# An RWKV-7 layer with a squared-ReLU feed-forward: stores of N on ScalarE's queue, moves of tokens three steps later, and v of chunk 5 fetched with its r

## The chip, the cores and the metric

The kernel runs on one core of one Trainium2 chip. The metric is the device time of a run in microseconds; the median of three runs is compared. Engines are named as in the profile: PE is TensorE (PEld its weight loads), DVE is VectorE, ACT is ScalarE, POOL is GpSimd, SP is SyncE. ACTq, SPq and POOLq are the sequencers of these engines when they issue DMAs.

## The reference

Four batches, eight heads, 768 time steps, head size 40. Each head has a 40 x 40 state that is updated step by step; its output goes, as 3072 tokens of 320 values, through a feed-forward layer of width 2048.

```python
for t in range(S):                       # S = 768; r, k, v, w, a, b: (4, 8, 768, 40)
    y[:, :, t] = einsum('bhd,bhde->bhe', rt, state)
    Sa = einsum('bhde,bhe->bhd', state, at)
    state = state * wt[:, :, None, :] - einsum('bhd,bhe->bhde', Sa, bt) + einsum('bhd,bhe->bhde', vt, kt)
x = y.transpose(0, 2, 1, 3).reshape(3072, 320)
h = maximum(x @ w_in, 0)                 # w_in (320, 2048)
out = (h * h) @ w_out                    # w_out (2048, 320)
```

## The kernel before

The sequence is cut into chunks of 128 steps; with four batches there are 24 chunks, in the order batch first, then time (`order`). `B` is 4. Within a chunk the recurrence becomes triangular systems that are solved by a matrix N and the inverse T of its diagonal blocks.

A chunk passes through these stages:

- `early(i)` (L342) reads w, a and b, forms the running products of decay (two scans and two reciprocals on DVE), and makes N: TensorE multiplies into PSUM, and ACT copies the result to the tile N (L373 to L377). The tile N has one buffer (L370), so the next chunk's copies wait until every store of this one has been read. Then N is stored to DRAM for the solver: in four pieces, `kept_q` for chunks 0 to 9 and `kept_d` for the others (L388); for chunks 2 to 9 also `kept_m`, two pieces (L390); for chunks from 2 on also `kept_n` (L392). The decay products go to `kept_e` (L367). Chunks 0 and 1 keep N's block and the decay products in SBUF; two of their four pieces are issued by ACT, everything else by SP.
- `take(u)` and `solve(u)` load the pieces of a unit of one, two or four chunks onto POOL, which solves for T (L448, L450) and stores it as `kept_t`.
- `rest(i)` in the first four slots, or the steps of `sorted_slot` later, loads k, the decay products `dec`, r, v, b, T (as `blocks` while the units are fine), N and `spares`, and forms kvT, A, rT, RV. For the fine units T is completed by two small products whose results ACT copies (`spares` L494, T L501).
- `chain(i)` (L604) is the recurrence itself: xr, two products with T, one with N between them, RX, and the output tile `tokens` (L669). After every second chunk, eight small DMAs (`moves`, L678 to L680) move rows within `tokens`, so that the feed-forward products fill 128 rows; `gathered` (L681) tells that they have been moved.
- The class `Ffn` multiplies tokens with `w_in` in quads (`thirds`, `whole`), squares on DVE and multiplies with `w_out` in quarters. The weights come in as pairs of 32-bit words and are put together by `rounding` (L258 to L277), on ACT and DVE, during the first five slots.

The order of instructions on each engine is written out by hand. A prologue (L827 to L868) prepares chunks 0 to 3. Then there is one slot for each chunk. Slots 0 to 3 use `woven` (L881): a `weave` of 12 steps interleaves the chain of chunk i, one or two `early` of later chunks (`ahead`: 4 and 5 in slot 0, 6 and 7 in slot 1, 8 and 9 in slot 2, 10 in slot 3, 11 and 12 in slot 4, 13 and 14 in slot 5, then one for each slot up to slot 14), `rest(i + 1)` and the rounding. Slots from 4 on use `sorted_slot` (L908), a fixed list of steps. The feed-forward part starts in slot 4.

DMAs that must not stand too early in SP's queue are put on a list with a number of steps:

```python
def later(fn, steps=2):
    line.append([steps, fn])

def tick():
    for entry in line:
        entry[0] -= 1
    while line and line[0][0] <= 0:
        line.pop(0)[1]()
```

`tick` runs once a step. The list is first in, first out: an entry with few steps waits for one with more that stands ahead of it. `store` is `later` with a DMA. `flush` ticks until the list is empty; it stands ahead of each `take`.

`fetch` takes the next tile of a ring: r has one tile, k and b two, v three. Chunk 5's r is fetched in `rest(4)` (L581) and its v at the end of slot 3 (L979), ahead of the other loads for chunk 5 (`loads`, L898). From slot 4 on the v of a chunk is fetched by L953.

Of the kernel before, what the change touches and what calls it, by code (L numbers as in the profile page):

```python
# [17 lines left out]
def kernel(  # L18
# [88 lines left out]
    def store(out_, in_, steps=2, queue=nc.sync):  # L107
        later(lambda: queue.dma_start(out=out_, in_=in_), steps)  # L108
# [233 lines left out]
    def early(i, g=None, apart=False):  # L342

        x_ = early_loaded.pop(i)
        dec = decays.next() if g is None else kept_here[i]
        if g is not None:
            nc.vector.memset(dec[:, :A_, :, MID:MID + 1], 1.0)
        up, down, aT = (dec[:, n] for n in (UP, DOWN, A_))
        wT = turn(x_["w"])
        yield  # L350
        for q in range(NP):
            nc.vector.tensor_tensor_scan(up[:, q, MID + 1:C + 1], wT[:, q, MID:], ones, 1.0, Alu.mult, Alu.mult)  # L352
            nc.vector.tensor_tensor_scan(down[:, q, MID - 1::-1], wT[:, q, MID - 1::-1], ones, 1.0, Alu.mult, Alu.mult)
        yield
        if not apart:
            bT_, aT_ = turn(x_["b"]), turn(x_["a"])
        nc.vector.reciprocal(down[:, :, MID + 1:C + 1], up[:, :, MID + 1:C + 1])  # L357
        nc.vector.reciprocal(up[:, :, :MID], down[:, :, :MID])
        yield
        if apart:  # L360
            bT_, aT_ = turn(x_["b"]), turn(x_["a"])
            yield
        bT = turned("bT", 1)
        nc.vector.tensor_tensor(bT, bT_, down[:, :, 1:C + 1], Alu.mult)
        nc.vector.tensor_tensor(aT[:, :, :C], aT_, up[:, :, :C], Alu.mult)  # L365
        if g is None:
            store(kept_e[i], dec[:USED])  # L367
        yield
        bb, c = order[i]
        t_ = new("N", [128, H, C], 1)  # L370
        for e, p_ in enumerate(products(bT, aT[:, :, :C])):
            plain, flip_ = t_[:, e:NP:2], t_[:, NP + e::2]
            nc.scalar.copy(plain, p_[:, ::2])  # L373
            for half in range(2):
                own_, other = (slice(n * HC, (n + 1) * HC) for n in (half, 1 - half))
                nc.scalar.copy(flip_[own_, :, own_], p_[other, 1::2, other])  # L376
            nc.scalar.copy(flip_[:HC, :, HC:], p_[:HC, 1::2, HC:])  # L377
        joins = lambda half: t_[half * HC:half * HC + Q, :, half * HC + Q:(half + 1) * HC]
        for half in range(2):
            for n in range(2):  # L380
                at = half * HC + n * Q
                if i < SMALL:
                    kept, to = kept_q[i, :, half, n], at + Q
                else:
                    u = unit_of[i]
                    kept, to = kept_d[u][i - units[u][0], :, half], (half + 1) * HC
                    kept = kept[:, n * Q * HC:n * Q * HC + Q * (to - at)].rearrange("h (s t) -> h s t", s=Q)
                store(kept.rearrange("h s t -> s h t"), t_[at:at + Q, :, at:to], 1, nc.scalar if g is not None and n else nc.sync)  # L388
            if i < SMALL and g is None:
                store(kept_m[i][half], joins(half), 1)  # L390
        if g is None:
            store(kept_n[i], t_[:HC, :, HC:], 1)  # L392
        else:
            g["dec"], g["N"] = dec, new("N21", [HC, H, HC], 2)
            nc.scalar.copy(g["N"], t_[:HC, :, HC:])
            g["joins"] = spare("joins", i)
            for half in range(2):
                nc.scalar.copy(g["joins"][half * HC:half * HC + Q], joins(half))
        yield
# [168 lines left out]
    def rest(i, g):  # L568
        begin(i, g)
        yield  # L570
        yield
        turn_k(i, g)
        joining = inverses(i, g) if i else iter(())
        if soon(i):
            next(joining, None)
        yield
        make_a(i, g)
        yield
        turn_rv(i, g)
        if i == B:  # L580
            fetch_next(i + 1, "r")  # L581
        yield
        decay_state(i, g)
        make_rv(i, g)
        if i and unit_of[i] < FINE:
            next(joining)
        yield
        turn_down(i, g)
        yield
        scale_kb(i, g)  # L590
        turn_state(i, g)
        yield
        yield from joining
        yield
# [9 lines left out]
    def chain(i, g):  # L604
        bb, c = order[i]
        st = states.tiles[bb]
        first, second_ = halves
        k_, b_, v_, rT = (g[x] for x in ("k", "b", "v", "rT"))

        x_ = psum(ps_c)[:, :DM].rearrange("t (h d) -> t h d", h=H)  # L610
        if c > 0:
            for f in range(2):
                for q in range(NP):
                    mm(x_[halves[f ^ q % 2], 2 * q:2 * q + 2], g["aT"][:, q, f * HC:(f + 1) * HC], st[:, q, :, :D], f == 0 and q < 2)
        for f in range(2):
            for n, (h, q, e, flip) in enumerate(heads):
                mm(x_[halves[f ^ flip], h], g["A"][e][:, q, f * HC:(f + 1) * HC], v_[:, h, :D], c == 0 and f == 0 and n < 2)
        xr = new("xr", [128, H, D], 1)
        nc.scalar.copy(xr, x_)  # L619
        yield  # L620
        T, N = g["T"], g["N"]
        xn = minus_x.next()

        def times_t(half):
            xs = psum(ps_c)[:, :NP * D].rearrange("p (n d) -> p n d", n=NP)
            for n, (h, q, e, flip) in enumerate(heads):
                rows = halves[half ^ flip]
                mm(xs[rows, n // 2], T[rows, order_of(h)], xr[rows, h], n < 2)
            for flip in range(2):
                nc.scalar.copy(flipped(xn)[halves[half], flip, :, :, :D], by_pair(xs[halves[half ^ flip]]))  # L630

        times_t(0)
        yield
        for h, q, e, flip in heads:
            mm(x_[halves[1 - flip], h], N[:, order_of(h)], xn[first, h, :D], False)
        for flip in range(2):
            nc.scalar.copy(flipped(xr)[halves[1 - flip], flip], flipped(x_)[halves[1 - flip], flip])
        yield
        times_t(1)
        yield  # L640
        p_ = psum(ps_c)
        for q in range(NP):
            nc.tensor.transpose(p_[:, q * 128:(q + 1) * 128], pair(xn, q), ident)  # L643
        xT = turned("xnT", 1)
        nc.scalar.copy(xT, quads(p_))
        yield
        y_ = quads(psum(ps_c))
        if c > 0:
            sd = g["sd"]
            for q in range(NP):  # L650
                mm(y_[:, q], sd[:, q].rearrange("p e d -> p (e d)"), rT[:, q], q == 0)
        yield
        rx = masked("RX", 2, xT, rT)
        yield

        for m_, rows in ((g["RV"], k_), (rx, b_)):
            for q in range(NP):
                for e in range(2):
                    mm(y_[e * DP:(e + 1) * DP, q], rows[:, 2 * q + e, :], m_[e][:, q], c == 0 and q == 0 and rows is k_)
        if c < NCH - 1:  # L660
            grown = psum(ps_w)[:, :NP * D].rearrange("p (q d) -> p q d", q=NP)
            for l_, r_ in ((k_, v_), (b_, xn)):
                for h in range(H):
                    mm(grown[h % 2 * DP:(h % 2 + 1) * DP, h // 2], l_[:, h, :], r_[:, h, :D], l_ is k_ and h < 2)
        n = i % GB
        if n == 0:
            tokens[i // GB] = new("tokens", [128, NP, GB * C], 2)
        t_ = tokens[i // GB][:, :, n * C:(n + 1) * C]
        nc.vector.tensor_tensor(t_, y_, g["up"][:, :, :C], Alu.mult)  # L669
        if c < NCH - 1:  # L670
            for e in range(2):
                rows = slice(e * DP, (e + 1) * DP)
                nc.vector.tensor_tensor(st[rows, :, e, :D], grown[rows], st[rows, :, e, :D], Alu.add)
            ended[bb] = new(f"end{bb}", [128, NP], 1)
            nc.scalar.copy(ended[bb], g["up"][:, :, C])
        if n == GB - 1:
            t_ = tokens[i // GB]
            for j, row, h, d, m_ in moves:  # L678
                at = (h % 2) * DP + d
                store(t_[row:row + m_, j], t_[at:at + m_, h // 2], 1)  # L680
            later(lambda: gathered.add(i // GB), 2)  # L681
        yield


# [283 lines left out]
    for i in range(len(order)):  # L968
# [4 lines left out]
        if i < B:  # L973
# [2 lines left out]
            n["chain"] = chain(i + 1, n)  # L976
            next(n["chain"])
            if i == B - 1:
                fetch_next(i + 2, "v")  # L979
                loads(i + 2)  # L980
        else:
            sorted_slot(i, g, ch)
# [37 lines left out]
```

## Time and profile before

| | us |
|---|---|
| median of 3 runs | 987.36 (986.25 to 987.77) |
| the profiled execution | 987.0 |
| its span | 985.3 |
| TensorE busy in the span | 875.7 (89%) |
| VectorE busy | 485.0 (49%) |
| ScalarE busy | 275.5 (28%) |
| GpSimd busy | 576.1 (58%) |
| SyncE's DMA queue (q1) | 259188 packets, 86.39 MB |
| ScalarE's DMA queue (q10) | 1088 packets, 0.13 MB |

The share of busy time is a mean over a stage of some 330 us in which the kernel loads, rounds and prepares, and a stage in which the feed-forward products fill TensorE. The output tile of the first chunk is written at 95.2 us, that of the last at 910.5 us. A wait in brackets is the idle time of an engine just ahead of an instruction, and what ended it. DMA issues on SPq and ACTq are not counted as busy.

### The profile page before, as it was taken

Reading aid. Unit: us, or ns where it says so; the run is one execution under the profiler, and the core shown is the slowest. Engines: PE = TensorE matmul, PEld = TensorE weight load, DVE = VectorE, ACT = ScalarE, POOL = GpSimd, SP = SyncE. Lnnn points to the kernel's source line nnn. Section 1 sums busy time; section 2 is a strip of 40 time slices with the busy share of each in tenths; the row PEclk is TensorE's granted clock in tenths of the full one; section 3 lists DMA queues with packets and bytes.
Section 4 is the critical chain, followed back from the end, with each engine's and each line's share of the span. In section 5 each row is a group of like instructions: output and inputs, shape, how many; then the busy total and the mean of one; then the engine's idle time right before and its main releaser. Section 6 shows DMA issues by size and latency. Waiting matters only on the chain.

```text
span 985.3 us, 21632 instructions
## 1 busy us (share of the span) xinstructions
PE 875.7 (89%) x8752; PEld 725.8 (74%) x8752; DVE 485.0 (49%) x868; ACT 275.5 (28%) x711; POOL 576.1 (58%) x989
## 2 busy tenths in 40 slices
PE   6447666667897999999999999999999999999998
PEld 4436555556685888888888888888888888887776
DVE  5528775758755454475446655632444423331111
ACT  3132423234323342332223232322222222222111
POOL 4788482836018985999976999959999800000000
PEclk9757565657698999999999999999999999999999
DMA  8987987894667579465588772585404364030000
GB/s 100 143 160 131 191 158 164 171 170 118 91 127 132 100 138 183 92 122 78 97 167 156 124 113 70 102 183 82 66 19 78 82 121 71 14 64 8 14 13 14
DMA packets 263431, 104.16 MB, mean 106 GB/s; under 512 B 246148, under 2 KB 252676, under 8 KB 261924
## 3 DMA queue, kind: packets, MB, share of 16 engines
q1 hardware_dynamic: 259188, 86.39, 50.9%
q0 software_dynamic: 3056, 16.26, 6.9%
q8 instruction: 69, 1.13, 0.5%
q10 hardware_dynamic: 1088, 0.13, 0.1%
q14 instruction: 30, 0.25, 0.1%
HBM read 70.11 MB, written 30.66 MB: 102 GB/s over the span
## 4 chain that ended last, share of the span: by engine, by line
PE 64%; SPq 1%; DVE 1%; DMA 1%; ACT 0%; issue 0%; ACTq 0%
PE ps_f L87 36%; PE ps_w L87 11%; PE ps_c L87 11%; PE ps_w L316 4%; PE ps_c L560 1%; PE ps_c L643 1%; PE ps_w L544 1%; DMA dec<-kept_e 1%; SPq L108 1%; SPq L464 0%; DMA tokens<-tokens 0%; DVE decay L357 0%; DVE state L535 0%; DVE RV L332 0%; ACT N L376 0%
## 5 line engine op out<-in xcount | busy, mean ns | idle before, releaser
L448 POOL TENSOR_TENSOR half_p<-half_n,half_t 128x120 f32<-128x120 f32 (+37 forms) x438 | 255.7, 584 | 84.4 <-DMA half_n<-kept_d 26.5
L450 POOL TENSOR_TENSOR half_t<-half_t,half_p 128x120 f32<-128x120 f32 (+37 forms) x438 | 275.9, 630 | 34.3
L87 PE MATMUL ps_f<-w_out,hid 128*128 128x320 f32 x768 | 217.4, 436 | 0.0
L87 PEld LDWEIGHTS ps_f<-w_out,hid 128*128 128x128 f32 x768 | 142.5, 190 | 54.6 <-issue 0.2
L87 PE MATMUL ps_f<-tokens,w_in 128*128 128x256 f32 x672 | 157.2, 388 | 0.0
L87 PEld LDWEIGHTS ps_f<-tokens,w_in 128*128 128x128 f32 x672 | 126.7, 194 | 17.9 <-issue 1.0
L734 DVE TENSOR_TENSOR hid<-hid 128x512 f32<-128x512 f32 x96 | 88.9, 963 | 50.2 <-ACT hid L727 49.7
L727 ACT ACTIVATE hid<-ps_f 128x512 f32<-128x512 f32 x84 | 50.2, 597 | 96.0 <-PE ps_f L87 96.0
L352 DVE TENSOR_TENSOR_SCAN decay<-ps_w,ones 128x64 f32<-128x64 f32 x88 | 23.8, 271 | 81.5 <-PE ps_w L316 81.5
L669 DVE TENSOR_TENSOR tokens<-ps_c,dec 128x512 f32<-128x512 f32 x24 | 16.5, 688 | 79.3 <-PE ps_c L87 79.3
L87 PE MATMUL ps_w<-decay,bT 40*128 40x128 f32 x352 | 30.0, 308 | 27.0 <-DVE decay L365 27.0
L373 ACT COPY N<-ps_w 128x256 f32<-128x256 f32 x48 | 17.7, 369 | 121.6 <-PE ps_w L87 74.7
L87 PEld LDWEIGHTS ps_w<-decay,bT 40*128 40x128 f32 x352 | 27.6, 213 | 30.2 <-issue 19.1
L510 DVE TENSOR_TENSOR kvT<-ps_w,dec 128x512 f32<-128x512 f32 x24 | 16.5, 688 | 66.9 <-ACT minus_x L630 33.9
L87 PE MATMUL ps_f<-tokens,w_third 64*128 64x256 f32 x336 | 46.9, 385 | 1.5 <-DVE w_out L266 1.5
L332 DVE TENSOR_TENSOR RX<-ps_w,upper 128x512 f32<-128x512 f32 x48 | 30.8, 683 | 32.1 <-PE ps_w L87 31.6
L332 DVE TENSOR_TENSOR RV<-ps_w,upper 128x512 f32<-128x512 f32 x48 | 30.9, 686 | 31.1 <-PE ps_w L87 30.8
L87 PEld LDWEIGHTS ps_c<-xr,T 64*64 64x64 f32 x768 | 30.7, 149 | 20.5 <-issue 15.0
L522 ACT COPY rT<-ps_w 128x512 f32<-128x512 f32 x24 | 14.0, 585 | 108.3 <-PE ps_w L316 108.3
L87 PE MATMUL ps_c<-xr,T 64*64 64x40 f32 x768 | 36.8, 243 | 3.6 <-ACT xr L619 1.6
L357 DVE RECIPROCAL decay<-decay 128x256 f32<-128x256 f32 x22 | 38.2, 1736 | 0.0
L532 DVE TENSOR_TENSOR f<-end,dec 128x4 f32<-128x4 f32 x20 | 5.1, 255 | 66.6 <-DMA dec<-kept_e 66.6
(130 smaller groups left out, 1411.7 us busy)
## 6 DMA issues: line engine op xcount, KB each, us to landing
kept_e<-decay SPq DMA_DIRECT2D x22, 633.8 KB
dec<-kept_e SPq DMA_DIRECT2D x22, 633.8 KB
hid<-in_moe_w_out_dram SPq DMA_DIRECT2D x16, 320.0 KB
half_n<-kept_d POOLq DMA_DIRECT2D x6, 768.0 KB, 10.3
in_w<-in_w_dram SPq DMA_DIRECT2D x24, 160.0 KB
in_ab<-in_b_dram SPq DMA_DIRECT2D x24, 160.0 KB
in_ab<-in_a_dram SPq DMA_DIRECT2D x24, 160.0 KB
in_k<-in_k_dram SPq DMA_DIRECT2D x24, 160.0 KB
```

Source lines behind the costliest of these rows:

```text
L87: nc.tensor.matmul(o, l_, r_, start=start, stop=True, skip_group_check=True)
L316: nc.tensor.transpose(p_[:, q * 128:(q + 1) * 128], pair(x_, q), ident)
L332: nc.vector.tensor_tensor(t_, p_, over4(upper), Alu.mult)
L352: nc.vector.tensor_tensor_scan(up[:, q, MID + 1:C + 1], wT[:, q, MID:], ones, 1.0, Alu.mult, Alu.mult)
L357: nc.vector.reciprocal(down[:, :, MID + 1:C + 1], up[:, :, MID + 1:C + 1])
L373: nc.scalar.copy(plain, p_[:, ::2])
L448: nc.gpsimd.tensor_tensor(p_, part[:, at:at + m_].unsqueeze(1).to_broadcast([128, n, m_]), t3[:, :n, s:s + 1].to_broadcast([128, n, m_]), ...
L450: nc.gpsimd.tensor_tensor(t3[:, :n, s + 1:], t3[:, :n, s + 1:], p_, Alu.subtract)
L510: nc.vector.tensor_tensor(kT, kT_, down[:, :, 1:C + 1], Alu.mult)
L669: nc.vector.tensor_tensor(t_, y_, g["up"][:, :, :C], Alu.mult)
L727: nc.scalar.activation(h_, p_.rearrange("p f t -> p (f t)"), Act.Relu)
L734: nc.vector.tensor_tensor(h_, h_, h_, Alu.mult)
```

## The change

All stores of N go to ACT's queue and are issued at once, behind ACT's copies of N, except for two of the four pieces of chunks 0 and 1, which stay on SP and are issued at once too. The moves of tokens are issued three steps after the chain's last step instead of one, and `gathered` is set after four steps instead of two; in `sorted_slot` the next chunk's `loads` stand between. The v of chunk 5 is fetched right behind its r in `rest(4)`, and no longer at the end of slot 3.

```diff
@@ in early() @@
-                store(kept.rearrange("h s t -> s h t"), t_[at:at + Q, :, at:to], 1, nc.scalar if g is not None and n else nc.sync)
+                (nc.sync if g is not None and not n else nc.scalar).dma_start(out=kept.rearrange("h s t -> s h t"), in_=t_[at:at + Q, :, at:to])
             if i < SMALL and g is None:
-                store(kept_m[i][half], joins(half), 1)
+                nc.scalar.dma_start(out=kept_m[i][half], in_=joins(half))
         if g is None:
-            store(kept_n[i], t_[:HC, :, HC:], 1)
+            nc.scalar.dma_start(out=kept_n[i], in_=t_[:HC, :, HC:])
@@ in rest() @@
         if i == B:
-            fetch_next(i + 1, "r")
+            fetch_next(i + 1, "r", "v")
@@ in chain() @@
-                store(t_[row:row + m_, j], t_[at:at + m_, h // 2], 1)
-            later(lambda: gathered.add(i // GB), 2)
+                store(t_[row:row + m_, j], t_[at:at + m_, h // 2], 3)
+            later(lambda: gathered.add(i // GB), 4)
@@ in the loop over the chunks @@
             if i == B - 1:
-                fetch_next(i + 2, "v")
                 loads(i + 2)
```

## The prediction

> **What bounds the kernel now.** I read the page's slices first, then a table of busy times by stage, then the list of TensorE instructions that had been waiting, stage by stage, and last the queues of SyncE and ScalarE beside them. On the page:
>
> ```profile
> PE   6447666667897999999999999999999999999998
> DMA  8987987894667579465588772585404364030000
> ```
>
> One slice is 24.6 us. TensorE has gaps up to slice 13 and none after; the transfers are dense in the same early stretch. The stage table (columns: stretch, length, then PE, PEld, DVE, ACT, POOL busy, clock, DMA share, GB/s):
>
> ```profile
> 155.00:215.00 60.00, 38.90 (x414) 32.99 (x410) 38.00 (x85) 21.29 (x60) 26.96 (x75) 0.56 0.86 169
> 330.00:466.00 136.00, 136.00 (x1616) 114.34 (x1616) 71.38 (x126) 45.11 (x122) 115.03 (x154) 1.00 0.69 122
> 500.00:700.00 200.00, 200.00 (x2085) 167.78 (x2083) 101.62 (x165) 55.54 (x146) 164.14 (x202) 1.00 0.63 116
> ```
>
> From 330 us on TensorE is busy all the time. What a queue gains there is worth nothing; what counts is when TensorE gets to 330 us. Before that the waits are these (start, duration, instruction, idle before it and what ended it):
>
> ```profile
> 103.44 1.44 PE L87 MATMUL ps_w<-blocks,spares 32*32 32x32 f32 x32 [3.22 <-ACT spares L494]
> 125.78 1.08 PE L316 MATMUL ps_w<-ident,in_w 128*128 128x128 f32 x4 [3.25 <-DMA in_w<-in_w_dram]
> 170.15 1.11 PE L316 MATMUL ps_w<-ident,in_k 128*128 128x128 f32 x4 [5.55 <-DMA in_k<-in_k_dram]
> 177.80 1.08 PE L316 MATMUL ps_w<-ident,in_w 128*128 128x128 f32 x4 [4.53 <-DMA in_w<-in_w_dram]
> 216.17 0.69 DVE L510 TENSOR_TENSOR kvT<-ps_w,dec 128x512 f32<-128x512 f32 x1 [3.61 <-DMA dec<-kept_e]
> 248.82 1.09 PE L316 MATMUL ps_w<-ident,in_v 128*128 128x128 f32 x4 [4.40 <-DMA in_v<-in_v_dram]
> 312.80 1.08 PE L316 MATMUL ps_w<-ident,in_w 128*128 128x128 f32 x4 [5.93 <-DMA in_w<-in_w_dram]
> ```
>
> Six late loads, and one wait (the first line, repeated at 152.77 and 200.89) on ScalarE, which copies N and then `spares` at the end of a slot. The loads are late because SyncE's queue issues in order and stores stand in front of them. The rows that price an issue:
>
> ```profile
> 15.80 0.84 ACTq L108 DMA_DIRECT2D kept_q<-N  x2
> 22.18 1.89 ACTq L108 DMA_DIRECT2D kept_q<-N  x2
> 24.11 0.58 ACT L522 COPY rT<-ps_w 128x512 f32<-128x512 f32 x1 [0.61 <-PE ps_w L316]
> 235.09 7.16 SPq L108 DMA_DIRECT2D tokens<-tokens  x8
> 468.75 1.82 SPq L108 DMA_DIRECT2D kept_d<-N  x4
> 470.67 0.56 SPq L108 DMA_DIRECT2D kept_n<-N  x1
> ```
>
> The third line matters most: that copy's input was ready at 23.46, yet it starts when the two ScalarE issues end (24.07). An issue on ScalarE blocks what stands behind it, 0.42 us each in a quiet moment, 0.95 us while SyncE is issuing loads.
>
> **What the skill says.** The Trainium skill, "DMA: Bandwidth & Descriptors", section "Issuing engines are not separate DMA queues": another issuing engine saves only its issue time, since all share 16 DMA engines. The trace agrees in part: issue and waiting on SyncE are what delays these loads. Same page, "Queues, rings and completion order": SyncE and ScalarE each own one row of rings, and a DMA engine serves the rows in turn; so stores on ScalarE no longer stand in front of loads, but take bandwidth beside them. The trace has two such queues (q1, and q10 with only 1088 packets), too few to show the sharing. Same page, "Anatomy of one DMA": a semaphore wait is served on the issuing sequencer before dispatch. The trace agrees: SyncE waited 72.7 us in total for N from ScalarE (14 times) and 35.6 us for PE reads.
>
> **The change, part by part.**
>
> *Stores of N.* SyncE loses 7 issues for each of chunks 2 to 9 (4 kept_q, 2 kept_m, 1 kept_n) and 5 for each of chunks 10 to 23; ScalarE gains them, straight behind its copies of N. Price of seven on ScalarE: 7 x 0.42 = 2.9 us at least (row at 15.80), 7 x 0.95 = 6.6 us at most (row at 22.18); I take 4.0, which is what SyncE needed for seven at 57.05 to 61.22. Price of five: 2.1 to 4.7, taken 2.5 (468.75 to 471.23). SyncE gains more than the issues, 6.1 to 7.9 us per chunk in the slots 1 and 2 (140.22 to 146.60, 154.83 to 160.97, 184.48 to 192.36), because it no longer waits for N there.
>
> The sum runs along the early slots. "+" is later than before.
>
> Slot 0, end: N of chunk 5 waits for kept_n of chunk 4 until 100.72; its product ended at 99.24, and with the stores issued about 12 us earlier it starts at 99.3: -1.4. Behind N stand 4.0 of issues, then `spares`, for which TensorE waits: +2.6.
>
> Slot 1: chunk 2's loads go out at about 102 instead of 110.14, so the wait at 125.78 is gone: 122.53 + 2.6 = 125.1, -0.6. N of chunk 6 ends at 124.86 + 2.6, plus 4.0, plus two rounding operations (1.1), plus rT (0.6): 133.2 against 130.5. The product that needs rT (2.1) ends at 135.3; VectorE took RX at 134.88: +0.4. VectorE's wait for `blocks` (1.0 at 138.35) goes: -0.6. N of chunk 7 and its issues: +3.4.
>
> Slot 2: k of chunk 3 goes out at 155.5 instead of 161.73 and lands at about 164, before TensorE comes (164.60 + 3.4). Late next is VectorE's decay, 168.13 + 3.4 = 171.5 against a product that began at 171.19: +0.3, so hardly anything of the 5.55 is kept. The wait of 4.53 at 177.80 is gone, but ScalarE, after N of chunk 8 (175.6 + 0.3), 4.0 of issues, 1.0 of rounding and rT, stands at 181.5 against 182.57: -1.1. N of chunk 9: +2.9.
>
> Slot 3: dec no longer late; VectorE is free at 212.56 + 2.9 = 215.5 against 216.17: -0.7. N of chunk 10, five issues: +1.8.
>
> *v of chunk 5.* It goes out at 226.6, behind r (226.12), instead of 245.40; its tile was chunk 2's, whose last reader is done. The wait of 4.40 goes. Late next is VectorE, dense with rounding until 249.22 + 1.8 = 251.0, where its scan began at 250.80: +0.2. Alone this part is worth 1.6 us, VectorE's idle time at that place.
>
> Slot 4: behind N of chunk 11 stand sd and two Relus; TensorE waits for the second at 282.61. Copies end 280.09, plus 2.5, plus sd and two Relus (1.6): 284.2. +1.7, together +1.9.
>
> Slot 5: v of chunk 6 and the loads of chunk 13 were held at 283.02 behind N of chunk 11, with DMA nearly idle (0.07 from 265 to 275); now they go out some 7 us earlier, and N of chunk 12 (305.13 to 309.14) leaves the queue. The w at 309.18 goes out at about 301 and the wait of 5.93 is gone: 306.87 + 1.9 = 308.8 against 312.80: **-4.0**.
>
> *From 330 us.* Five issues per slot up to slot 14. At slot 9 N ends at 469.30; plus 2.6, sd and the first Relu (1.1): 473.0, and the product that reuses that bank starts at 475.42. The 2.4 us of slack hide them; five issues at 0.95 would leave a fraction of a us in each of nine slots.
>
> *Moves of tokens.* Eight issues, 6.3 to 7.2 us of SyncE, after every second chunk. In slots 1 and 3 three steps are used up by the last two steps of the interleaved work, so they still stand ahead of the next loads; only the order with kept_e changes. I cost that at nothing (bounds -1 to +1: dec of chunk 5 goes out 3.7 us earlier, without TensorE waiting for it). From slot 5 on dec, k, b and T go ahead of them; TensorE is full, so nothing is gained. The feed-forward part reads them a whole slot (over 30 us) later, which covers the delay. r, the output store and kept_e now stand behind the moves; each has most of a slot of slack.
>
> *Prologue.* N of chunk 3 waited 12.0 us for kept_n and will not, but POOL solves without a gap from 25 to 109 us and TensorE waits for it. Nothing, bounds -2 to +1.
>
> **Sum.** The profiled execution took 987.0 us (span 985.3 and 1.7 around it), 0.36 below the median of 987.36. 987.0 - 4.0 = 983.0; against the median 983.4. I say 983.3.
>
> **The rivals.**
> *ScalarE becomes the bound (slower).* At the ends of slots 0 to 3 its issues stand in front of `spares`. In slots 0 and 2 SyncE is then issuing k, dec, r, v and b, the situation of the row at 22.18. With 6.6 and 4.7 the same sum gives about +13. It is roughly linear: 4.0 gives -4, 6.6 gives +13, so from 4.6 us for seven the change loses. At 5.4 it is +5: 992. For it: the 1.89 row, and DMA shares above 0.8. Against: the 0.84 row, and ScalarE's own ring being empty.
> *Issues are cheap.* At 2.9 and 2.1 the same sum gives about -9: 978. For it only the row at 15.80.
> *The loads don't land earlier.* The share is 0.86 in slots 1 to 3; if the DMA engines, not the queue's order, set the landing, the waits stay and swallow ScalarE's issues: 987. Against it: the share drops to 0.4 to 0.6 just ahead of the late loads.
>
> **Chances.** A measurement here tells about 0.2% (2 us) from no change. Forecast 0.42 (0.38 faster, 0.04 same); ScalarE bound 0.34 (0.32 slower, 0.02 same); cheap issues 0.10, faster; loads not earlier 0.14 (0.02 faster, 0.08 same, 0.04 slower). Faster 0.50, same 0.14, slower 0.36. The range goes from the cheap end, 977, to 994, where seven issues cost 5.7.
>
> **What the new profile would show.** Right: no waits for in_k, in_w or in_v between 120 and 320 us; kept_q, kept_m and kept_n on ACTq at about 0.55 us each; longer waits for `spares` at the slots' ends; TensorE continuous from about 326 us. Wrong: issues above 0.65 us, `spares` waits above 7 us, or the load waits still there.

## The result, and the profile after

The kernel became slower: 1001.81 us median of 4 runs (999.26 to 1003.71) against 987.57 us, ratio 1.0145, 95% interval 1.012 to 1.017. The profiled execution of after took 1003.71 us, its span is 1002.0 us. The forecast was 983.3 us, faster. Ratios here and below are of fast runs alone; the slow ones among all runs, two of e2 and two of before beside e12 (1007.75 to 2861.41 us), stay out of them.

The page's slices first (one slice is 25.05 us here), PE and DMA:

```profile
PE   6544573758599999999999999999999999999998
...
DMA  9986786957738567665659764566414354220000
```

In sum the first 13 slices have become emptier for both, and TensorE is full behind them as before. The table by stage (stretch, length, then PE, PEld, DVE, ACT, POOL busy, clock, DMA share, GB/s):

```profile
155.00:215.00 60.00, 34.90 (x380) 30.64 (x380) 39.65 (x81) 19.27 (x55) 25.95 (x72) 0.58 0.68 142
500.00:700.00 200.00, 200.00 (x2094) 168.07 (x2094) 105.71 (x177) 55.16 (x146) 164.04 (x203) 1.00 0.64 121
```

In the first stretch the DMA share fell from 0.86 to 0.68 and TensorE lost 4 us. The full stage has the same rate as before. So the loss lies ahead of it: the product rT,kvT that TensorE began at 349.88 in before begins 16.4 us later, at 366.27, and the end of the span is 16.7 us later. Of these 16.7 us, 9.5 are idle time of TensorE and 7.2 busy time (882.9 against 875.7 us; ends of matmuls are modelled, and why it grew is left open). In the early stages these instructions of TensorE had waited (start, duration, instruction, idle before it and what ended it):

```profile
96.02 2.08 PE L87 MATMUL ps_w<-rT,kvT 40*128 40x128 f32 x16 [13.39 <-ACT kvT L523]
...
117.05 1.45 PE L87 MATMUL ps_w<-blocks,spares 32*32 32x32 f32 x32 [5.09 <-ACT spares L494]
...
171.47 1.45 PE L87 MATMUL ps_w<-blocks,spares 32*32 32x32 f32 x32 [9.44 <-ACT spares L494]
...
231.47 2.08 PE L87 MATMUL ps_w<-dec,kvT 40*128 40x128 f32 x16 [1.11 <-DVE kvT L510]
```

The waits for late loads are gone, as forecast: TensorE waited 25.2 us for loads in before and never in after. In their place it waits for ScalarE: for `spares` and kvT together 47.1 us instead of 10.7. The longest is the 13.39 us for kvT in slot 0. Before, that product waited for nothing, and ScalarE's copy of rT ahead of it only for TensorE:

```profile
82.55 0.58 ACT L522 COPY rT<-ps_w 128x512 f32<-128x512 f32 x1 [2.98 <-PE ps_w L316]
...
85.17 1.92 PE L87 MATMUL ps_w<-rT,kvT 40*128 40x128 f32 x16
```

It is now 10.9 us late, although the slot had started 2.4 us early (decay,bT of chunk 4 at 73.68 instead of 76.09). What ScalarE did there in after (ACTq is its sequencer issuing DMAs):

```profile
76.91 0.26 ACT L377 COPY N<-ps_w 64x128 f32<-64x128 f32 x1
80.06 1.04 ACTq L388 DMA_DIRECT2D kept_q<-N  x2
81.23 0.58 ACTq L390 DMA_DIRECT2D kept_m<-N  x1
85.11 6.80 ACTq L388 DMA_DIRECT2D kept_q<-N  x2
92.13 1.67 ACTq L390 DMA_DIRECT2D kept_m<-N  x1
93.89 0.95 ACTq L392 DMA_DIRECT2D kept_n<-N  x1
94.89 0.59 ACT L522 COPY rT<-ps_w 128x512 f32<-128x512 f32 x1 [17.73 <-DMA kept_q<-N]
```

N of chunk 4 (N(4) from here on) is copied by 77.17. Its seven stores stand there until 94.84, and rT behind them for 17.7 us. The rows are groups: the two `kept_q` of "6.80" took 0.33 and 0.31 us to issue; the rest is time between them. The seven issues took 4.6 us in all, the longest 1.67; the other 13.1 us are waits ahead of them. The seven of chunk 5, later in the same slot, look quite different:

```profile
112.73 0.31 ACTq L388 DMA_DIRECT2D kept_q<-N  x1
...
114.25 1.06 ACTq L388 DMA_DIRECT2D kept_q<-N  x2
...
116.02 0.58 ACTq L392 DMA_DIRECT2D kept_n<-N  x1
```

That is 3.9 us, what the prediction had put on seven. Same stores, same engine, 3.9 us and 17.7 us: most of the difference is not the price of an issue.

That price is not the same everywhere, though. Behind the copies of N(7), which end at 163.34, and N(8) single issues took over 2 us:

```profile
164.37 2.21 ACTq L388 DMA_DIRECT2D kept_q<-N  x2
166.61 2.12 ACTq L390 DMA_DIRECT2D kept_m<-N  x1
...
191.66 2.57 ACTq L390 DMA_DIRECT2D kept_m<-N  x1
```

Of the 7.7 us from the last copy of N(7) to `spares` at 171.06, 1.7 are a wait, for `kept_e` of chunk 7; its seven issues, of which the first began ahead of the last copy, took 6.2 us. N(8)'s seven took 6.5, N(5)'s, N(6)'s and N(9)'s 3.5, 4.4 and 4.1. Beside the long issues of N(7), SyncE's issues of `in_k` and `dec` took 1.61 and 2.56 us. What makes an issue long no run here separates.

What N(4)'s stores wait for stands in the program that the kernel is built into. A completion semaphore is the counter that the program has a DMA raise when it is done. All 591 DMAs of SyncE and ScalarE share eight of them, given out in strict rotation in the order of the program; before each DMA there is a wait until the one eight places ahead of it, which has the same semaphore, has landed (written out for 554 of the 583 that have one ahead). Around N(4) (place, semaphore, issuing engine, DMA | what it waits for):

```
65 DMAHW0 SP         in_w  <- in_w_dram   | #57
66 DMAHW1 SP         in_ab <- in_b_dram   | #58
67 DMAHW2 SP         in_ab <- in_a_dram   | #59
68 DMAHW3 SP         kept_e4 <- decay     | #60
69 DMAHW4 Activation kept_q <- N          | #61 SP blocks
70 DMAHW5 Activation kept_q <- N          | #62 SP blocks
71 DMAHW6 Activation kept_m4 <- N         | #63 SP blocks
72 DMAHW7 Activation kept_q <- N          | #64 SP blocks
73 DMAHW0 Activation kept_q <- N          | #65 SP in_w
74 DMAHW1 Activation kept_m4 <- N         | #66 SP in_ab (b)
75 DMAHW2 Activation kept_n4 <- N         | #67 SP in_ab (a)
```

The stores read nothing of `blocks` or of chunk 6's w, b and a. SyncE issues these loads from 77.77 to 84.96, with `blocks` waiting for the solver, and the chain that ended last has the landing as a piece of its own, with ScalarE's issues right behind it:

```profile
79.72 0.62 SPq L470
81.08 11.03 DMA in_ab<-in_b_dram
92.13 1.67 ACTq L390
...
95.37 0.60 ACT kvT L523
96.02 2.13 PE ps_w L87 x16
```

The Trainium skill, "DMA: Bandwidth & Descriptors", section "Why a DMA increments its semaphore by 16 and not by 1", gives a reason for such a wait: with two DMAs in flight on one semaphore, a wait can pass before the first has wholly landed. No run here shows that case. In this kernel such a wait on SyncE holds up other DMAs; on ScalarE it holds up compute, here rT.

### The profile page after: what moved, and what is told of

Its sections match the earlier page's. It is cut to its first block, busy times and chain, and to the rows that moved or that the text cites. A ratio compares the mean times of both kernels' runs of the same rounds, so it can differ in the third digit from the quotient of the medians.

```text
span 1002.0 us, 21585 instructions
## 1 busy us (share of the span) xinstructions
PE 882.9 (88%) x8752; PEld 732.8 (73%) x8752; DVE 482.4 (48%) x868; ACT 275.0 (27%) x711; POOL 577.9 (58%) x989
## 4 chain that ended last, share of the span: by engine, by line
PE 73%; DVE 9%; DMA 4%; issue 3%; ACT 3%; POOL 3%; ACTq 2%; SPq 1%; DVEq 0%; POOLq 0%
PE ps_f L87 39%; PE ps_w L87 15%; PE ps_c L87 13%; PE ps_w L316 4%; DMA in_ab<-in_b_dram 1%; DVE decay L357 1%; ACTq L388 1%; POOL half_t L450 1%; PE ps_c L560 1%; POOL half_p L448 1%; PE ps_c L643 1%; DMA w_out<-in_moe_w_in_dram 1%; DVE decay L358 1%; PE ps_w L544 1%; ACT N L376 1%
## 5 line engine op out<-in xcount | busy, mean ns | idle before, releaser
L87 PEld LDWEIGHTS ps_f<-tokens,w_in 128*128 128x128 f32 x672 | 126.0, 192 | 17.7 <-issue 1.0
L87 PE MATMUL ps_w<-decay,bT 40*128 40x128 f32 x352 | 32.3, 325 | 26.0 <-DVE decay L365 22.5
L87 PE MATMUL ps_w<-rT,kvT 40*128 40x128 f32 x384 | 33.1, 317 | 22.9 <-ACT kvT L523 20.6
L87 PEld LDWEIGHTS ps_w<-decay,bT 40*128 40x128 f32 x352 | 30.0, 231 | 29.4 <-issue 15.5
L373 ACT COPY N<-ps_w 128x256 f32<-128x256 f32 x48 | 17.7, 369 | 115.1 <-PE ps_w L87 105.1
L87 PEld LDWEIGHTS ps_w<-rT,kvT 40*128 40x128 f32 x384 | 27.9, 216 | 25.6 <-ACT kvT L523 22.2
```

The costliest lines, as they stand in the source:

```text
L87: nc.tensor.matmul(o, l_, r_, start=start, stop=True, skip_group_check=True)
```

## The experiments

Theories: **landing** (a store on ScalarE waits until the DMA eight places ahead of it has landed), **issue price** (each issue costs ScalarE 0.6 to 0.95 us wherever it is) and **shared bandwidth** (stores on ScalarE's ring slow the loads). Times are set against runs of before on the same chip, with medians of 989.4 to 989.8 us there.

| run | median us | ratio to before (95%) |
|---|---|---|
| e1 stores of N alone | 1007.16 | 1.0181 (1.0145 to 1.0217) |
| e2 moves and v | 987.94 | 0.9981 (0.997 to 0.9992) |
| e3 three marks | 994.79 | 1.005 (1.003 to 1.0069) |
| e4 after, loads behind N(4)'s stores | 998.69 | 1.0089 (1.0054 to 1.0124) |
| e5 e4, two of N(7)'s stores on SyncE | 997.42 | 1.0091 (1.0057 to 1.0124) |
| e6 ScalarE stores chunks 2, 3 only | 990.75 | 1.0008 (0.9996 to 1.0021) |
| e7 e4, chunks 5, 7, 9 on SyncE | 1000.8 | 1.0111 (1.0076 to 1.0146) |
| e8 ScalarE stores chunks 10 to 23 only | 988.79 | 0.9995 (0.9982 to 1.0008) |
| e9 marks, with loads behind | 990.33 | 1.0008 (0.9998 to 1.0018) |
| e10 ScalarE stores 4 to 9, three steps later | 988.62 | 0.9999 (0.9986 to 1.0012) |
| e11 the same for 4, 6, 8 | 987.56 | 0.9982 (0.9971 to 0.9992) |
| e12 v alone | 988.1 | 0.9986 (0.9975 to 0.9997) |

**e1, which part loses.** The diff of before with only the hunks of `early`.

> Kernel before with only the stores of N moved to ScalarE (no later moves, v of chunk 5 as before). Landing theory (a store on ScalarE waits until the DMA eight places ahead of it in the program has landed): rT of slot 0 is late by about 11 us again, for moves and v come after it; in slot 1 the moves of tokens stand further ahead, so N(7)'s seven take about 4 us instead of 8.2. In all +11 to +15 us on before. Issue-price theory (each issue costs ScalarE 0.6 to 0.95 us wherever it is): the loss is spread over the slots, +6 to +14 in all, slot 0 no more than +4. If the loss is not the stores' at all, about 0.

The whole loss is the stores': +17.9 us, above the 11 to 15 expected and above after's, with overlapping intervals. In slot 0 the rT,kvT product waits 11.48 us (13.39 in after). One part of the expectation failed: with the moves further ahead, N(7) is no cheaper. TensorE waits 9.63 us for `spares` at the end of slot 1 (9.44 in after), so the later moves are not to blame for it.

**e2, the other two parts.** Before with the hunks of `rest`, `chain` and the loop.

> Kernel before with only the other two parts: moves of tokens three steps later and v of chunk 5 with its r; the stores of N stay on SyncE. Prediction's steps: -1.6 us (v's wait of 4.40 gone, 1.6 of it kept), moves nothing: 985.8. If the moves do harm (later issue in front of N(7)'s stores or of the next loads), +2 to +5.

-1.9 us (interval -3.0 to -0.8). The later moves do no harm.

**e3, the wait without the stores.** Before, with three DMAs of 64 bytes on ScalarE.

```diff
             store(kept_n[i], t_[:HC, :, HC:], 1)
+            if i == 4:
+                for m_ in range(3):
+                    mark = dram.tile([1, 16], FP32, tag=f"mark{m_}", name=f"mark{m_}")
+                    nc.scalar.dma_start(out=mark, in_=ident[:1, :16])
```

> Kernel before, stores of N on SyncE as they were; behind ScalarE's copies of N of chunk 4 three added DMAs of 64 bytes (a row of ident to scratch). They move no data to speak of and need nothing that is late. Landing theory: the third stands eight places behind the load of in_w of chunk 6, which SyncE issues at 82.5 us and which lands some 5 to 8 us later; ScalarE's copy of rT, at 82.55 in before, then starts at 88 to 91, and the kernel is +4 to +8 us slower. Issue-price theory: 3 x 0.45 to 3 x 0.95 = 1.4 to 2.9 us behind copies that end at 79.6, where rT has 3.0 us of slack: rT where it was, kernel the same. Shared-bandwidth theory: the same, nothing.

ScalarE in e3:

```profile
83.77 11.19 ACTq L396 DMA_DIRECT2D mark<-ident  x3
95.00 0.59 ACT L526 COPY rT<-ps_w 128x512 f32<-128x512 f32 x1 [17.58 <-DMA in_w<-in_w_dram]
```

192 bytes hold rT as long as all seven stores do, and the trace names what they wait for: in_w. The first two marks, whose places have `blocks` ahead, were issued at 83.77 and 84.81, beside SyncE's loads, in 0.46 and 0.23 us; the third alone waited until 94.75. The kernel is 5 us slower (the profiled execution 10). For the wait in slot 0 this rules out the bandwidth of the stores, and the number and price of the issues. The landing took longer than expected, 11 us after in_w was issued at 83.59, in a stretch where the DMA engines are full (the view gives a share of 1.11 from 83.6 to 95).

Of after's 14.2 us this wait alone explains about a third: rT was as late here, and the kernel lost 5.

**e9, its counterpart.** The marks of e3, with the three loads emitted later, so that they stand behind N(4)'s stores in the program. (e4 has the same edit.)

```diff
+        if i == 5:
+            for _ in range(2):
+                next(gen)
+                yield
         if i + 1 < len(order) and i + 1 not in early_loaded:
             load_early(i + 1)
```

> Kernel of the three-marks run (before, plus three 64-byte DMAs on ScalarE behind N of chunk 4), with the early loads of chunk 6 emitted two pieces later, behind N(4)'s stores. The marks are the same; now they stand eight places behind the loads of chunk 5, landed long ago, and one of blocks. Landing theory: the wait of 17.6 us for in_w is gone, rT follows the copies of N within 4 to 9 us (the third mark waits for blocks), and the kernel is within 3 us of before. If instead any DMA issued by ScalarE at that place is held up by what runs on SyncE's queue, rT stays at about 95 us and the kernel at +5.

```profile
81.29 0.26 ACT L377 COPY N<-ps_w 64x128 f32<-64x128 f32 x1
83.74 0.22 ACTq L396 DMA_DIRECT2D mark<-ident  x1
84.00 0.59 ACT L526 COPY rT<-ps_w 128x512 f32<-128x512 f32 x1 [2.46 <-DMA blocks<-kept_t]
```

The same marks now cost 2.46 us, the landing of blocks, which stands in the third one's place; two had been issued between the copies. rT follows sooner than the 4 to 9 us expected, and the kernel is within 0.2% of before. What the third mark costs is set by what stands eight places ahead of it.

**e4, the same in the changed kernel.**

> Kernel after, with one change: the three early loads (w, b, a) of chunk 6 are emitted two pieces of chunk 5's preparation later, so that they stand behind N(4)'s seven stores in the program instead of ahead; same instructions on the same engines. Landing theory: ScalarE's seven now wait for blocks and older loads only, which land by about 83 us, and rT starts at 83 to 85 instead of 94.89; the kernel comes down by 8 to 11 us to 991 to 994. Issue-price theory: seven issues are still there, 1001.8. Shared-bandwidth theory: fewer loads beside the stores, at most 2 us.

In e4's program only places 65 to 88 differ from after's. rT starts at 85.98, where 83 to 85 was expected and 94.89 had been: the last stores still wait for blocks. At the end of slot 0 TensorE is 9.2 us earlier than in after (`spares` product at 107.82 instead of 117.05). In all e4 is 0.56% better, some 5.5 us, set across two chips (1 to 10 us with both intervals): less than the 8 to 11 expected. By the end of slot 1 more than 4 of the 9.2 were gone again, most of them at N(6):

```profile
140.84 2.08 PE L87 MATMUL ps_w<-rT,kvT 40*128 40x128 f32 x16 [4.64 <-ACT kvT L523]
...
166.92 1.45 PE L87 MATMUL ps_w<-blocks,spares 32*32 32x32 f32 x32 [9.66 <-ACT spares L494]
```

N(6)'s stores have the load of chunk 2's v, those of chunk 7's w, b, a and three of weights eight places ahead, and ScalarE now reaches them sooner after their issue (TensorE waited 1.17 us there in after). The second line is N(7).

**e5, what N(7) waits for.** In e4, `kept_n` and the second `kept_m` of chunk 7 on SyncE.

> Kernel of the loads-behind run (after, with chunk 6's early loads behind N(4)'s stores), with two of N(7)'s seven stores (kept_n and the second kept_m) back on SyncE. In that run the last of the seven waited from 161.6 to 165.9 us, which the landing theory puts down to kept_e of chunk 7 (issued at 159.60, eight DMAs ahead of it). With two fewer on ScalarE none of its five has kept_e in its place: landing theory: spares of slot 1 starts about 4 us earlier (near 162 after copies that end at 158.6), and SyncE takes over the wait, so that k of chunk 3 may go out late; kernel -2 to -4 against that run. Issue-price theory: two issues fewer, -1.1.

```profile
162.30 1.45 PE L87 MATMUL ps_w<-blocks,spares 32*32 32x32 f32 x32 [5.07 <-ACT spares L500]
...
181.31 1.09 PE L316 MATMUL ps_w<-ident,in_w 128*128 128x128 f32 x4 [1.52 <-DMA in_w<-in_w_dram]
```

The `spares` product comes 4.6 us sooner (166.92 to 162.30), against 1.1 for two issues: in e4 N(7)'s last store had waited until 165.84 for `kept_e` of chunk 7. Then it is given back: SyncE takes the wait over, a load is late again, and with N(8)'s stores behind it 1.1 us are left at the next `spares` product, at 213.75. The medians do not tell e5 from e4, where 2 to 4 us had been expected.

**e6 and e8, which chunks lose.** In `early`, `nc.scalar` at once for the chunks named, else the old `store`; moves and v as in after.

> Kernel after with the stores of N on ScalarE for chunks 2 and 3 alone (the two prepared in the prologue, before the woven slots); chunks 4 to 23 back on SyncE, one step later, as before. Moves and v as in after. Landing theory: no store on ScalarE is left in the slots, so rT of slot 0 is not late; the first spares product comes at about 55 as in after, of which the weights' rounding leaves 1 to 3 us; with v's 1.6 the kernel is at 983 to 987 (0 to -4 on before). Issue-price theory: about the same, -2.

> Kernel after with the stores of N on ScalarE for chunks 10 to 23 alone (five each); chunks 2 to 9 on SyncE as before; moves and v as in after. The prediction's steps for slots 3 to 5: +1.8, +1.7 and -4.0 with v: -0.6 to -2 on the moves-and-v run; from 330 us nothing. Landing theory: some of these stores stand behind loads too, but TensorE is covered: between -2 and +2 on before; the loss of after comes from chunks 4 to 9.

Both are the same as before within 0.2%. e6 misses its range of 983 to 987 and lies 0.27% above e2, with intervals that do not meet: the stores of chunks 2 and 3 add some 1 to 4 us, compared across two chips. e8's 0.14% over e2 cannot be told from nothing. Most of the loss is that of chunks 4 to 9. The 7.0 us by which after's first `spares` product was early (55.05 against 62.09) bring nothing: ScalarE then waits 5.89 us for weights, and the second xr,T product is only 1.3 us early (68.12).

**e7, a miss.** e4 with the stores of 5, 7 and 9 on SyncE.

> Kernel of the loads-behind run with the stores of N of chunks 5, 7 and 9 (those that stand right before the copy to spares at a slot's end) back on SyncE; ScalarE keeps chunks 2, 3, 4, 6, 8 and 10 to 23. Landing theory: the waits left on ScalarE are those of N(4) behind blocks (2 us) and of N(6) behind the loads of slot 1 (6 us); against before +2 to +5. Issue-price theory: 3 x 4.0 taken off the critical places of the loads-behind run: -12 on it, 3 us below before.

+11 us on before. The copies to `spares` were free of stores as planned (1.73 us of waiting instead of 5 to 10), but both kinds of wait are now there at once: chunks 4, 6 and 8 hold TensorE for 5.41, 4.48 and 5.67 us at rT,kvT, and the late loads of the kernel before are back:

```profile
130.19 1.08 PE L316 MATMUL ps_w<-ident,in_w 128*128 128x128 f32 x4 [2.86 <-DMA in_w<-in_w_dram]
```

k of chunk 3 is waited for 5.10 us, at 177.84.

So SyncE's relief, which the prediction counted, is real; the expectation for e7 had left it out. e7 doesn't separate issues from waits.

**e10 and e11, the stores where ScalarE is idle.** Moves and v as in after; the stores of chunks 4 to 9 (e11: 4, 6, 8) on ScalarE from a list of their own, three steps later, so that rT, kvT and T stand ahead of them; the others on SyncE.

```diff
+    def store_n(i, out_, in_, queue=nc.sync):
+        if 4 <= i < 10:                      # e11: i in (4, 6, 8)
+            held.append([3, lambda: nc.scalar.dma_start(out=out_, in_=in_)])
+        else:
+            store(out_, in_, 1, queue)
```

> Moves and v as in after; the stores of N of chunks 4 to 9 on ScalarE, but three steps behind the copies of N (for chunks 5, 7 and 9 at the end of the slot, behind spares and T); chunks 2, 3 and 10 to 23 on SyncE as before. Landing theory: for chunks 4, 6 and 8 the waits fall where ScalarE is idle (92 to 100 us in slot 0), so rT is not late; SyncE is relieved and the late loads of slots 1 and 2 are gone; the stores of 5, 7 and 9 still stand in front of xr, about 4 us each: 980 to 990 against 989.4. Issue-price theory: the same six packs of seven on ScalarE as in after: +6 to +12.

> As the run with stores three steps later, but for chunks 4, 6 and 8 alone; 5, 7 and 9 on SyncE as before. Landing theory: nothing of ScalarE's waits lies on the path any more; half of SyncE's relief is kept: -2 to -6 on before. Issue-price theory: +3 to +6.

The loss is gone with the same six packs of stores on ScalarE: e10 is at 0.9999. In e11 N(4)'s stores lie on ScalarE from 86.58 to 98.49, and rT has started at 79.22. This shows that the place on ScalarE decides; it does not separate waits from issues, as both now lie where nothing on the path stands behind them. No gain is left over e2, though (e11 is 1.8 us below before, just short of the 2 to 6 expected). N has one buffer, and in the program N(5)'s copies wait for all stores of N(4). They began at 100.72 in before and begin at 106.99 in e11, and TensorE then waits at the end of slot 0:

```profile
109.72 1.45 PE L87 MATMUL ps_w<-blocks,spares 32*32 32x32 f32 x32 [10.53 <-ACT spares L506]
```

In e10 it waits 8.07 us there, and three times some 3 us more behind the stores of chunks 5, 7 and 9. (That N(4)'s stores landed last is not shown: the trace puts the end of that wait down to `kept_e`.) e2, e11 and e12 are the fastest versions found, and cannot be told apart.

**e12, v alone.** Before with the hunks of `rest` and the loop.

> Kernel before with v of chunk 5 fetched with its r, and nothing else (stores of N on SyncE, moves of tokens one step later as before). The prediction's step: v alone is worth 1.6 us, VectorE's idle time at that place, so 987.9 against 989.5, and the run of moves and v (-0.19%) is then all v's. If the later moves bring part of it, v alone is nearer to 0; a wait for in_v that is still there would say that it was the transfer, not the queue.

-1.4 us (interval -2.5 to -0.3) against 1.6 forecast. The wait for in_v is gone, and behind it TensorE waits 4.80 us for VectorE (1.53 in before). The moves' own share, e2 against e12, cannot be told from nothing.

## Why the prediction was wrong

The step that failed is the cost of the stores on ScalarE: "I take 4.0" for each pack (the seven stores of one chunk's N), put in front of `spares` and rT as an issue price. For N(4) the sum had no term at all, and nothing in it stood for a wait of ScalarE for SyncE's loads, and in slot 0 that is what counts: N(4)'s pack took 17.7 us, 13.1 of them waits for landings. As an issue price 4.0 was right for N(5), N(6) and N(9) (3.5, 4.4, 4.1; the row that it came from, 57.05 to 61.22, gives 4.2), and too low for N(7) and N(8) (6.2 and 6.5, N(7) with 1.7 of waiting more). Five took 2.4 at 382.54, against 2.5.

The prediction's figures add up along the slots, so they are compared here with the delay of TensorE against before at the same instruction.

- *Slot 0, end.* Forecast +2.6, measured +13.6 (117.05 against 103.44). Ahead of rT ScalarE had been idle for 2.98 us in before, enough for most of an issue price of 4.0, not for 17.7.
- *Slot 1, end.* Forecast +3.4, so 0.8 more; measured +18.7 (171.47 against 152.77), so 5.1 more. The wait for w went as forecast; most of the excess is N(7)'s pack, 7.7 instead of 4.0.
- *Slots 2 and 3.* Forecast from +3.4 to +0.2; measured from +18.7 to +16.7 at the first thirds product of slot 4 (272.04 against 255.31). The waits for k, w, dec and v went; the 1.11 left at dec,kvT is for VectorE.
- *Slot 4.* The Relu: forecast +1.7 (its figures, 284.2 against 282.61, give 1.6), measured +2.7 (to +19.45 at 302.06).
- *Slot 5.* Forecast from +1.9 to -4.0, so -5.9; measured -4.7 (to +14.8 at 347.79). The wait of 5.93 is gone.
- *v of chunk 5.* Right: -1.4 against -1.6 (e12), and VectorE late next.
- *From 330 us.* Nearly right: +1.6 from slot 5 to 6, forecast nothing; then flat.
- *Moves.* Right: no effect that the runs can tell. *Prologue.* 7 us early, of which 1.3 are left after the weights; within the bounds given.

How the 14.2 us split among the packs is known only in part. The wait of N(4) is shown (e3, e9, e4) and is worth about 5 us at the end of the kernel. The rest comes from the other packs of chunks 4 to 9 (e6, e8), as issues and as waits together; e5 shows a wait for N(7) in e4's program, and no run takes the two apart for the others.

The rival "ScalarE becomes the bound" had the side right and the mechanism in part. It scaled the issue price to 0.95 us each while SyncE is issuing loads. N(7) and N(8) come near it (0.89 and 0.92 on average), though not as a price of every issue: the row at 22.18 was one of 0.40 and one of 1.46, and of after's 130 issues on ScalarE 17 took over 0.65 us, up to 2.57, while the median is 0.46. It missed the waits, the largest single piece, so that its +13 comes near the measured +14.2 is partly luck. Of the signs that the prediction named, the load waits gone and issues of about 0.55 us came true for most; issues above 0.65 us and a `spares` wait above 7 us (9.44), its signs of being wrong, came true as well. The largest wait, for kvT, was not on the list. That stores on ScalarE no longer stand in front of loads was right; now the loads stand in front of them.

The skill's sentence that I leaned on, "DMA: Bandwidth & Descriptors", section "Issuing engines are not separate DMA queues", says that issuing from several engines only saves the time of the sequencer. In e3 it also added something: through the semaphores that this program shares between the queues, a wait of 17.6 us for three DMAs of 64 bytes.

The trace of before had a hint that I passed over. SyncE's waits there (engine and line, what it waited for, total, times, longest) have pairs that share no data:

```profile
SPq L249 <- DMA kept_q<-N: 2.8, 2, 1.8
...
SPq L108 <- DMA w_out<-in_moe_w_in_dram: 2.8, 4, 2.0
```

A load of weights waits for a store of N, and stores at L108 wait for a load of weights, which none of them reads. That points to something shared, and the program shows what.

## What to carry to other kernels

Before moving a DMA to the queue of an engine that computes, list what the program makes it wait for, the reuse of its completion semaphore included, and ask when that lands. In this kernel the price was the latest landing (17.6 us in e3) or the issues themselves (3.5 to 6.5 us for seven), never a fixed 4.0. A wait in the trace between two DMAs that share no data is the sign to look for. If such a DMA must go to a computing engine, put it where that engine is idle (e10), and see that its source buffer isn't needed before: in e10 and e11 TensorE waited 8.07 and 10.53 us for it.

## What the runs showed that was not expected

- The DMAs of two engines are coupled through eight semaphores in rotation: in this program the wait follows the place in it, not the queue. Moving three loads by a few places turned a wait of 17.58 us into one of 2.46 (e3, e9).
- A load of 160 KB issued at 83.59 us was waited for until close to 95, 11 us, where the DMA engines are full. Seven issues on ScalarE took 3.5 to 6.5 us.
- Relief on one queue and the waits on another are separate accounts: e7 pays both, with three packs of stores on ScalarE. e10, with six, has neither the wait at rT nor most late loads, and pays instead for the one buffer of N.
